# Attention and feed-forward kernel: more buffers for attention, and the first feed-forward chunk placed ahead of the second batch's attention

## The chip, the cores and the metric

The kernel runs on one core of one Trainium2 chip. The metric is device microseconds (us) of one execution. The clock that was granted to the tensor engine and the busy times come from a profile of one execution; the span in a profile is about 1.7 us shorter than the time of the same run.

## The reference

Four batches of eight heads, 768 tokens and 64 features go through attention that keeps four sink tokens and a window of 128. The heads are then joined to 512 features per token, and a gated feed-forward block with RMS norm follows.

```python
scores = scale * np.matmul(q, k.transpose(0, 1, 3, 2))
keep = is_sink | in_window                      # first 4 keys, or 0 <= query - key < 128
a = softmax(np.where(keep, scores, -1e9))
x = (a @ v).transpose(0, 2, 1, 3).reshape(B * S, H * D)      # 3072 x 512

xn = x / np.sqrt(np.mean(x * x, -1, keepdims=True) + 1e-6) * rms_g
g, val = xn @ w_gate, xn @ w_val                # 512 -> 1536
out = (g * sigmoid(g) * val) @ w_out            # 1536 -> 512
```

## The kernel before

Attention works on pairs of heads, four pairs to a batch. The feed-forward part works on 12 chunks of 256 tokens, three to a batch. Inputs are float32 in memory and are cast to bf16 by the loads; all those loads are issued by GpSimd, in one queue. A list scheduler puts the instructions of each engine in a fixed order, by the order in which the program emits them and by what each needs. On its engine each instruction then waits its turn.

```python
ld = ctx.enter_context(tc.tile_pool(name="ld", bufs=2))     # q, k as loaded
c1 = ctx.enter_context(tc.tile_pool(name="c1", bufs=2))     # qT, kT
vp = ctx.enter_context(tc.tile_pool(name="vp", bufs=3))     # v with a column of ones
ptp = ctx.enter_context(tc.tile_pool(name="ptp", bufs=3))   # probabilities
# ...
def attention_pair(b, hp_idx):
    # ... load q, k (2 heads each) and v; transpose q and k on the tensor engine
    vaug = vp.tile([P, NT, D + 1], BF16, tag="vaug")
    nc.gpsimd.memset(vaug[:, :, D : D + 1], 1.0)
    nc.gpsimd.dma_start(out=vaug[:, :, 0:D], in_=vv)
    # ... scores into s_ps, exp on ScalarE, mask on VectorE, product with v into o_ps
    # ... divide by the sum: x_all[:, b * NT : (b + 1) * NT, h * D : (h + 1) * D]

def stats_batch(b):      # 6 blocks: bn_stats, bn_aggr; then mean square, Sqrt, reciprocal
    ...

def ffn_chunk(c):
    # ... xn = x_all * rstd; 8 transposes into xnT_ps; xnT = xnT_ps * rms_g
    hTs[0] = emit_silu(emit_gv(0))          # 4 gate and 4 value matmuls, then the gating
    hTs[1] = emit_silu(emit_gv(1))
    for f in range(NFB):                    # 12 blocks
        if f + 2 < NFB:
            hTs[f + 2] = emit_silu(emit_gv(f + 2))
        emit_out(f, hTs.pop(f))             # 2 matmuls with wo

attention_batch(0)
stats_batch(0)
load_weights()                              # wg, wv, wo: one GpSimd load each
for b in range(1, B):
    attention_batch(b)
    stats_batch(b)
    ffn_batch(b - 1)
ffn_batch(B - 1)
```

The softmax here doesn't subtract the row's maximum and nothing guards it: scores larger than these inputs give would overflow.

Of the kernel before, what the change touches and what calls it, by code (L numbers as in the profile page):

```python
# [10 lines left out]
FP32 = mybir.dt.float32  # L11
BF16 = mybir.dt.bfloat16
ACT = mybir.ActivationFunctionType
ALU = mybir.AluOpType
# [3 lines left out]
def kernel(  # L18
# [33 lines left out]
    assert S % TC == 0  # L52
    TPC = TC // P
    CPB = S // TC
    SCALE = 1.0 / float(D) ** 0.5
    EPS = 1e-6

# [66 lines left out]
    x_all = xpool.tile([P, TBLK, DM], FP32)  # L124

    ld = ctx.enter_context(tc.tile_pool(name="ld", bufs=2))
    c1 = ctx.enter_context(tc.tile_pool(name="c1", bufs=2))
    vp = ctx.enter_context(tc.tile_pool(name="vp", bufs=3))
    ptp = ctx.enter_context(tc.tile_pool(name="ptp", bufs=3))
    smallp = ctx.enter_context(tc.tile_pool(name="smallp", bufs=3))  # L130
    apS = ctx.enter_context(tc.tile_pool(name="apS", bufs=2, space=bass.MemoryType.PSUM))
    apO = ctx.enter_context(tc.tile_pool(name="apO", bufs=1, space=bass.MemoryType.PSUM))
# [5 lines left out]
    fps = ctx.enter_context(tc.tile_pool(name="fps", bufs=3, space=bass.MemoryType.PSUM))  # L138
    fpo = ctx.enter_context(tc.tile_pool(name="fpo", bufs=1, space=bass.MemoryType.PSUM))

    def attention_pair(b: int, hp_idx: int):
        h0 = 2 * hp_idx
        q_b16 = ld.tile([P, NT, 2, D], BF16, tag="qb")
        k_b16 = ld.tile([P, NT, 2, D], BF16, tag="kb")
        for hh in range(2):
            qv = q[b, h0 + hh].rearrange("(t p) d -> p t d", p=P)
            kv = k[b, h0 + hh].rearrange("(t p) d -> p t d", p=P)
            nc.gpsimd.dma_start(out=q_b16[:, :, hh, :], in_=qv)  # L148
            nc.gpsimd.dma_start(out=k_b16[:, :, hh, :], in_=kv)  # L149

        make_consts()
        vaugs = []
        for hh in range(2):
            vv = v[b, h0 + hh].rearrange("(t p) d -> p t d", p=P)
# [3 lines that stand above are left out]
            vaugs.append(vaug)  # L158

        qT_ps = apS.tile([P, NT * P], BF16, tag="sps")  # L160
        for t in range(NT):
            nc.tensor.transpose(  # L162
                qT_ps[:, t * P : (t + 1) * P],
                q_b16[:, t, :, :].rearrange("p hh d -> p (hh d)"),
                ident[:],
            )
        qT2 = c1.tile([P, NT * P], BF16, tag="qT")
        nc.vector.tensor_copy(out=qT2[:], in_=qT_ps[:])
        kT_ps = apS.tile([P, NT * P], BF16, tag="sps")
        for t in range(NT):  # L170
            nc.tensor.transpose(  # L171
                kT_ps[:, t * P : (t + 1) * P],
                k_b16[:, t, :, :].rearrange("p hh d -> p (hh d)"),
                ident[:],
            )
        kT2 = c1.tile([P, NT * P], BF16, tag="kT")
        nc.vector.tensor_copy(out=kT2[:], in_=kT_ps[:])

        far = (NT - 2) * P
        pts, ptsinks = [], []  # L180
        for hh in range(2):
            pb = hh * D
            qT = qT2[pb : pb + D, :]
            kT = kT2[pb : pb + D, :]
            ssk_ps = apS.tile([NS, far], FP32, tag="sps")
            nc.tensor.matmul(  # L186
                ssk_ps[:],
                lhsT=kT[:, 0:NS],
                rhs=qT[:, 2 * P : NT * P],
                start=True,  # L190
                stop=True,
            )
            ptsink = ptp.tile([P, far], BF16, tag="ptsink")
            nc.gpsimd.memset(ptsink[:], 0.0)  # L194
            nc.scalar.activation(out=ptsink[0:NS, :], in_=ssk_ps[:], func=ACT.Exp, scale=SCALE)  # L195
            ptsinks.append(ptsink)
            pt_all = ptp.tile([P, NT * 2 * P], BF16, tag="ptall")
            pts.append(pt_all)

        for kp in range(KPAIRS):  # L200
            kb0 = 2 * kp
            nkb = 2 if kb0 + 1 < NT else 1
            spp = []
            for hh in range(2):
                pb = hh * D
                qT = qT2[pb : pb + D, :]
                kT = kT2[pb : pb + D, :]
                s_ps = apS.tile([P, 4 * P], FP32, tag="sps")
                cols = 0
                for i in range(nkb):  # L210
                    kb = kb0 + i
                    ncols = 2 * P if kb < NT - 1 else P
                    nc.tensor.matmul(  # L213
                        s_ps[:, i * 2 * P : i * 2 * P + ncols],
                        lhsT=kT[:, kb * P : (kb + 1) * P],
                        rhs=qT[:, kb * P : kb * P + ncols],
                        start=True,
                        stop=True,
                    )
                    cols = i * 2 * P + ncols  # L220
                spp.append((s_ps, cols))
            mk = maskA if kp == 0 else maskB
            for hh in range(2):
                s_ps, cols = spp[hh]
                base = kb0 * 2 * P
                nc.scalar.activation(  # L226
                    out=pts[hh][:, base : base + cols],
                    in_=s_ps[:, 0:cols],
                    func=ACT.Exp,
                    scale=SCALE,  # L230
                )
                nc.vector.tensor_tensor(  # L232
                    out=pts[hh][:, base : base + cols],
                    in0=pts[hh][:, base : base + cols],
                    in1=mk[:, 0:cols],
                    op=ALU.mult,
                )

        for hh in range(2):
            h = h0 + hh  # L240
            pt_all = pts[hh]
            ptsink = ptsinks[hh]
            vaug = vaugs[hh]
            o_ps = apO.tile([P, NT, D + 1], FP32, tag="ops")
            for jq in range(NT):
                nc.tensor.matmul(  # L246
                    o_ps[:, jq, :],
                    lhsT=pt_all[:, jq * 2 * P : jq * 2 * P + P],
                    rhs=vaug[:, jq, :],
                    start=True,  # L250
                    stop=(jq == 0),
                )
                if jq >= 1:
                    nc.tensor.matmul(  # L254
                        o_ps[:, jq, :],
                        lhsT=pt_all[:, (jq - 1) * 2 * P + P : jq * 2 * P],
                        rhs=vaug[:, jq - 1, :],
                        start=False,
                        stop=(jq == 1),
                    )  # L260
                if jq >= 2:
                    nc.tensor.matmul(  # L262
                        o_ps[:, jq, :],
                        lhsT=ptsink[:, (jq - 2) * P : (jq - 1) * P],
                        rhs=vaug[:, 0, :],
                        start=False,
                        stop=True,
                    )
            r = smallp.tile([P, NT, 1], FP32, tag="recip")
            nc.vector.reciprocal(out=r[:], in_=o_ps[:, :, D : D + 1])  # L270
            nc.vector.tensor_tensor(
                out=x_all[:, b * NT : (b + 1) * NT, h * D : (h + 1) * D],
                in0=o_ps[:, :, 0:D],
                in1=r[:].to_broadcast((P, NT, D)),
                op=ALU.mult,
            )

    def attention_batch(b: int):
        for hp_idx in range(H // 2):
            attention_pair(b, hp_idx)  # L280

    rstd_all = xpool.tile([P, TBLK, 1], FP32)

    def stats_batch(b: int):
        mv = fsm.tile([P, NT, nc.vector.BN_AGGR_DIM], FP32, tag="mv")
        for t in range(NT):
            stats = fsm.tile([P, nc.vector.BN_STATS_DIM], FP32, tag="stats")
            nc.vector.bn_stats(out=stats[:], in_=x_all[:, b * NT + t, :])  # L288
            nc.vector.bn_aggr(out=mv[:, t, :], in_=stats[:])
        msq = fsm.tile([P, NT, 1], FP32, tag="msq")  # L290
        nc.vector.tensor_tensor(
            out=msq[:], in0=mv[:, :, 0:1], in1=mv[:, :, 0:1], op=ALU.mult
        )
        nc.vector.tensor_tensor(out=msq[:], in0=msq[:], in1=mv[:, :, 1:2], op=ALU.add)
        nc.vector.tensor_scalar_add(out=msq[:], in0=msq[:], scalar1=EPS)
        nc.scalar.activation(out=msq[:], in_=msq[:], func=ACT.Sqrt)
        nc.vector.reciprocal(out=rstd_all[:, b * NT : (b + 1) * NT, :], in_=msq[:])

    def ffn_chunk(c: int):
        tb0 = c * TPC  # L300
# [25 lines left out]
        def emit_gv(f):  # L326
            gv_ps = fps.tile([P, 2, TC], FP32, tag="gv")
            for kci in range(NKC):
                nc.tensor.matmul(  # L329
                    gv_ps[:, 0, :],  # L330
                    lhsT=wg_bf[:, kci, f * P : (f + 1) * P],
                    rhs=xnT[:, kci, :],
                    start=(kci == 0),
                    stop=(kci == NKC - 1),
                )
            for kci in range(NKC):
                nc.tensor.matmul(  # L337
                    gv_ps[:, 1, :],
# [51 lines left out]
            r0 = row0 + tbi * P  # L390
            nc.sync.dma_start(out=out[r0 : r0 + P, :], in_=o_sb[:])

    def ffn_batch(b: int):
        for sub in range(CPB):
            ffn_chunk(b * CPB + sub)

    attention_batch(0)
    stats_batch(0)
    load_weights()
    for b in range(1, B):  # L400
        attention_batch(b)
        stats_batch(b)
        ffn_batch(b - 1)
    ffn_batch(B - 1)


# [33 lines left out]
```

## Time and profile before

| Reading of the kernel before | value | view |
|---|---|---|
| time, median of the first 3 runs | 334.79 us (333.09 to 336.43) | runs |
| span of the profiled run | 331.0 us | page |
| tensor engine busy | 286.6 us, 87% | page, part 1 |
| idle for the q of batch 1 | 8.43 us | timeline |
| that q, from issue to landing | 17.0 us | chain of waits |
| first gate matmul of chunk 0 | 60.42 us | timeline |
| attention of batch 1 with chunk 0 | 60.42 to 100.05 us, 39.6 us | timeline |
| one chunk alone | 16.83 us | timeline |

These are lines of the profile page. Part 1 gives the busy time of each engine (PE is the tensor engine, PEld its loading of weights, DVE the vector engine, ACT ScalarE, POOL GpSimd, each with its count of instructions). Part 2 cuts the span into 40 slices of 8.3 us and gives the busy tenths of each; PEclk is the clock that was granted to the tensor engine, in tenths of full speed.

```profile
PE 286.6 (87%) x2432; PEld 186.9 (56%) x2432; DVE 227.5 (69%) x616; ACT 146.6 (44%) x309; POOL 102.2 (31%) x186
...
PE   1687641999987999999988999999779999999993
...
PEclk9999999999999999999999999999999999999998
DMA  7999999979968010399890010931010101010101
```

After the seventh slice the tensor engine is nearly full. The 4 and the 1 in slices six and seven are the hole that the change is aimed at, and the DMA line shows the queues nearly full until then. The hole itself is seen in the timeline of the tensor engine. Its columns are start, length, operation, output and inputs, sizes, count, and in brackets the idle time before the line and what ended it.

```profile
47.30 0.24 PE L262 MATMUL o_ps<-vaug,ptsink 128*128 128x65 bf16 x1
55.97 0.80 PE L162 MATMUL qT_ps<-ident,q_b 128*128 128x128 bf16 x6 [8.43 <-DMA q_b<-in_q_dram]
...
58.68 1.24 PE L311 MATMUL xnT_ps<-ident,xn 128*128 128x128 bf16 x8
60.42 1.01 PE L329 MATMUL gv_ps<-xnT,wg_bf 128*128 128x256 bf16 x4 [0.49 <-DVE xnT L318]
```

Attention of batch 0 ends at 47.5 us. The next instruction in the fixed order transposes a q that has not landed. Only behind it come the transposes of chunk 0 (xnT_ps) and its first gate matmul. Why that q is late shows in the timeline of GpSimd, which issues the loads.

```profile
24.97 0.86 POOL L113 DMA_DIRECT2D wg_bf<-in_moe_w_gate_dram  x1
...
27.99 0.12 POOL L156 MEMSET vaug<- 128x6 bf16 x1 [0.83 <-PE o_ps L262]
...
29.31 0.76 POOL L116 DMA_DIRECT2D wv_bf<-in_moe_w_val_dram  x1
34.91 0.12 POOL L156 MEMSET vaug<- 128x6 bf16 x1 [4.84 <-PE o_ps L262]
...
36.23 1.02 POOL L119 DMA_DIRECT2D wo_bf<-in_moe_w_out_dram  x1
...
38.86 0.86 POOL L148 DMA_DIRECT2D q_b<-in_q_dram  x1
```

GpSimd twice stops for a v buffer, until the tensor engine has finished with an old one (o_ps). With three buffers the last v loads of batch 0, and everything behind them, are issued late and among the weights. The list of loads gives size and time from issue to landing.

```profile
wg_bf<-in_moe_w_gate_dram POOLq DMA_DIRECT2D x1, 1536.0 KB, 12.1
wv_bf<-in_moe_w_val_dram POOLq DMA_DIRECT2D x1, 1536.0 KB, 16.4
wo_bf<-in_moe_w_out_dram POOLq DMA_DIRECT2D x1, 1536.0 KB, 17.7
```

The weights land at 37.1, 45.7 and 53.9 us, 8.6 and 8.2 us apart, with v loads of batch 0 between them in the queue, and q of batch 1 lands right behind them, at 55.8 us. In the chain of waits (start, length, what) it is one piece.

```profile
38.86 16.97 DMA q_b<-in_q_dram
```

Last, matmuls of one size (256 columns) in three windows: 24 to 32 us, inside attention of batch 0 and long before the hole, then 60 to 67 us and 70 to 80 us. The columns after the count are busy time, mean nanoseconds of one, and idle time before.

```profile
L213 PE MATMUL s_ps<-qT,kT 64*128 64x256 bf16 x8 | 2.4, 394 | 1.8 <-ACT pt_all L226 1.8
...
L329 PE MATMUL gv_ps<-xnT,wg_bf 128*128 128x256 bf16 x8 | 2.4, 404 | 0.5 <-DVE xnT L318 0.5
...
L213 PE MATMUL s_ps<-qT,kT 64*128 64x256 bf16 x14 | 2.9, 273 | 0.3 <-ACT ptsink L195 0.2
L329 PE MATMUL gv_ps<-xnT,wg_bf 128*128 128x256 bf16 x12 | 2.3, 275 | 0.0
```

After the hole a gate matmul takes 404 ns, later 275 ns.

### The profile page before, as it was taken

How to read it: one execution, taken by the hardware profiler on the slowest of the kernel's cores; microseconds unless marked ns; L12 is line 12 of the kernel's file. 1: busy time of each engine (PE TensorE's matmuls, PEld its weight loads, DVE VectorE, ACT ScalarE, POOL GpSimd, SP SyncE). 2: the span in 40 equal slices, each digit the busy share in tenths (PEclk: the TensorE clock that was granted, in tenths of full speed). 3: DMA queues.
4: the chain of work that ended last, by engine and by line, in shares of the span. 5: the costliest groups of instructions: out<-in, count | busy, mean ns of one | idle time of the engine just before them, and what ended most of it. 6: DMA issues, size and time to landing. Idle time of an engine off the chain costs nothing.

```text
span 331.0 us, 6385 instructions
## 1 busy us (share of the span) xinstructions
PE 286.6 (87%) x2432; PEld 186.9 (56%) x2432; DVE 227.5 (69%) x616; ACT 146.6 (44%) x309; POOL 102.2 (31%) x186
## 2 busy tenths in 40 slices
PE   1687641999987999999988999999779999999993
PEld 1243321365565767655756677655557676767771
DVE  0354455677798686797887776987966767676662
ACT  0654340567636253466454353666343333242422
POOL 8995644477751000487430000830000000000000
PEclk9999999999999999999999999999999999999998
DMA  7999999979968010399890010931010101010101
GB/s 48 71 98 168 205 203 170 78 51 81 75 42 107 2 63 2 71 103 78 57 107 5 2 63 0 137 28 12 2 65 0 63 2 63 3 64 2 63 2 63
DMA packets 81886, 20.86 MB, mean 63 GB/s; under 512 B 76224, under 2 KB 77760, under 8 KB 81856
## 3 DMA queue, kind: packets, MB, share of 16 engines
q0 software_dynamic: 77872, 14.16, 52.9%
q1 hardware_dynamic: 3984, 6.30, 5.2%
q8 instruction: 19, 0.31, 0.4%
q14 instruction: 11, 0.09, 0.1%
HBM read 28.31 MB, written 6.29 MB: 105 GB/s over the span
## 4 chain that ended last, share of the span: by engine, by line
PE 51%; DVE 23%; ACT 10%; DMA 6%; POOL 4%; issue 3%; ACTq 0%; POOLq 0%
PE gv_ps L329 11%; PE gv_ps L337 10%; PE out_ps L371 10%; DVE hT L359 9%; DVE u_sb L350 9%; PE s_ps L213 9%; ACT t_sb L348 7%; DMA q_b<-in_q_dram 6%; DVE stats L288 3%; PE o_ps L246 3%; ACT ptsink L195 2%; PE qT_ps L162 2%; PE kT_ps L171 2%; PE ssk_ps L186 2%; PE o_ps L254 2%
## 5 line engine op out<-in xcount | busy, mean ns | idle before, releaser
L348 ACT ACTIVATE t_sb<-gv_ps 128x256 bf16<-128x256 f32 x144 | 55.0, 384 | 108.3 <-DVE hT L359 70.5
L329 PE MATMUL gv_ps<-xnT,wg_bf 128*128 128x256 bf16 x576 | 92.7, 275 | 2.2 <-DVE xnT L318 2.0
L371 PE MATMUL out_ps<-wo_bf,hT 128*128 128x512 bf16 x288 | 86.0, 380 | 6.5 <-DVE hT L359 5.9
L337 PE MATMUL gv_ps<-xnT,wv_bf 128*128 128x256 bf16 x576 | 90.8, 274 | 0.0
L350 DVE SCALAR_TENSOR_TENSOR u_sb<-t_sb,gv_ps 128x256 bf16<-128x256 bf16 x144 | 59.9, 418 | 44.5 <-ACT t_sb L348 44.0
L329 PEld LDWEIGHTS <-wg_bf 128*128 128x128 bf16 x576 | 54.4, 98 | 35.0 <-issue 7.6
L359 DVE SCALAR_TENSOR_TENSOR hT<-u_sb,gv_ps 128x256 bf16<-128x256 bf16 x144 | 59.7, 418 | 3.4
L337 PEld LDWEIGHTS <-wv_bf 128*128 128x128 bf16 x576 | 55.3, 98 | 9.7 <-issue 3.5
L226 ACT ACTIVATE pt_all<-s_ps 128x512 bf16<-128x512 f32 (+1 forms) x96 | 52.8, 562 | 14.7 <-PE s_ps L213 13.3
L213 PE MATMUL s_ps<-qT,kT 64*128 64x256 bf16 x192 | 40.1, 301 | 9.4 <-ACT ptsink L195 5.1
L371 PEld LDWEIGHTS <-hT 128*128 128x128 bf16 x288 | 25.8, 98 | 19.3 <-DVE hT L359 12.7
L156 POOL MEMSET vaug<- 128x6 bf16 x32 | 4.8, 152 | 96.6 <-PE o_ps L262 96.6
L232 DVE TENSOR_TENSOR pt_all<-pt_all,maskB 128x512 bf16<-128x512 bf16 (+1 forms) x64 | 24.8, 390 | 12.3 <-ACT pt_all L226 11.4
L148 POOL DMA_DIRECT2D q_b<-in_q_dram x32 | 27.5, 859 | 18.0 <-PE qT_ps L162 12.0
L213 PEld LDWEIGHTS <-kT 64*128 64x128 bf16 x192 | 11.9, 97 | 32.0 <-issue 29.5
L149 POOL DMA_DIRECT2D k_b<-in_k_dram x32 | 27.3, 852 | 5.4 <-DMA wo_bf<-in_moe_w_out_dram 5.4
L246 PE MATMUL o_ps<-vaug,pt_all 128*128 128x65 bf16 x192 | 25.2, 209 | 2.6 <-DMA vaug<-in_v_dram 2.4
L157 POOL DMA_DIRECT2D vaug<-in_v_dram x32 | 26.9, 840 | 0.9 <-POOL ptsink L194 0.9
L195 ACT ACTIVATE ptsink<-ssk_ps 4x512 bf16<-4x512 f32 x32 | 17.5, 579 | 18.0 <-PE ssk_ps L186 17.8
L246 PEld LDWEIGHTS <-pt_all 128*128 128x128 bf16 x192 | 17.5, 105 | 14.0 <-DVE pt_all L232 5.8
L232 DVE TENSOR_TENSOR pt_all<-pt_all,maskA 128x512 bf16<-128x512 bf16 x32 | 13.6, 425 | 16.7 <-ACT pt_all L226 16.5
L254 PE MATMUL o_ps<-vaug,pt_all 128*128 128x65 bf16 x160 | 23.7, 207 | 0.0
(47 smaller groups left out, 247.1 us busy)
## 6 DMA issues: line engine op xcount, KB each, us to landing
out_dram<-o_sb SPq DMA_DIRECT2D x24, 256.0 KB, 2.2
q_b<-in_q_dram POOLq DMA_DIRECT2D x32, 96.0 KB, 3.3
k_b<-in_k_dram POOLq DMA_DIRECT2D x32, 96.0 KB, 3.4
vaug<-in_v_dram POOLq DMA_DIRECT2D x32, 96.0 KB, 3.3
wg_bf<-in_moe_w_gate_dram POOLq DMA_DIRECT2D x1, 1536.0 KB, 12.1
wv_bf<-in_moe_w_val_dram POOLq DMA_DIRECT2D x1, 1536.0 KB, 16.4
wo_bf<-in_moe_w_out_dram POOLq DMA_DIRECT2D x1, 1536.0 KB, 17.7
rmsg<-in_moe_rms_g_dram SPq DMA_DIRECT2D x1, 2.0 KB, 2.2
```

The source lines that it names most:

```text
L148: nc.gpsimd.dma_start(out=q_b16[:, :, hh, :], in_=qv)
L213: nc.tensor.matmul(s_ps[:, i * 2 * P : i * 2 * P + ncols], lhsT=kT[:, kb * P : (kb + 1) * P], rhs=qT[:, kb * P : kb * P + ncols], start=Tr ...
L226: nc.scalar.activation(out=pts[hh][:, base : base + cols], in_=s_ps[:, 0:cols], func=ACT.Exp, scale=SCALE,)
L232: nc.vector.tensor_tensor(out=pts[hh][:, base : base + cols], in0=pts[hh][:, base : base + cols], in1=mk[:, 0:cols], op=ALU.mult,)
L246: nc.tensor.matmul(o_ps[:, jq, :], lhsT=pt_all[:, jq * 2 * P : jq * 2 * P + P], rhs=vaug[:, jq, :], start=True, stop=(jq == 0),)
L254: nc.tensor.matmul(o_ps[:, jq, :], lhsT=pt_all[:, (jq - 1) * 2 * P + P : jq * 2 * P], rhs=vaug[:, jq - 1, :], start=False, stop=(jq == 1),)
L329: nc.tensor.matmul(gv_ps[:, 0, :], lhsT=wg_bf[:, kci, f * P : (f + 1) * P], rhs=xnT[:, kci, :], start=(kci == 0), stop=(kci == NKC - 1),)
L337: nc.tensor.matmul(gv_ps[:, 1, :], lhsT=wv_bf[:, kci, f * P : (f + 1) * P], rhs=xnT[:, kci, :], start=(kci == 0), stop=(kci == NKC - 1),)
L348: nc.scalar.activation(out=t_sb[:], in_=gv_ps[:, 0, :], func=ACT.Tanh, scale=0.5)
L350: nc.vector.scalar_tensor_tensor(out=u_sb[:], in0=t_sb[:], scalar=1.0, in1=gv_ps[:, 1, :], op0=ALU.add, op1=ALU.mult,)
L359: nc.vector.scalar_tensor_tensor(out=hT[:], in0=u_sb[:], scalar=0.5, in1=gv_ps[:, 0, :], op0=ALU.mult, op1=ALU.mult,)
L371: nc.tensor.matmul(out_ps[:, tbi, :], lhsT=hT[:, tbi * P : (tbi + 1) * P], rhs=wo_bf[:, f, :], start=(f == 0), stop=(f == NFB - 1),)
```

## The change

The intent is to let attention of batch 0 run without waiting for buffers, and to fill the hole with chunk 0, which needs no q. Three edits carry it. The pools get 4 and 9 buffers, so that all of batch 0's v loads can be issued ahead of the weights. Chunk 0 is emitted before attention of batch 1, and an ordering edge puts the tensor engine's work for attention of batch 1 behind the first gate matmul of chunk 0's sixth block. The statistics of batch 0 are taken in two parts of 2 and 4 blocks, so that chunk 0 (2 blocks) could start earlier. The diff also cuts the attention function into three functions, which does the same work and is left out here.

```diff
-    c1 = ctx.enter_context(tc.tile_pool(name="c1", bufs=2))
-    vp = ctx.enter_context(tc.tile_pool(name="vp", bufs=3))
-    ptp = ctx.enter_context(tc.tile_pool(name="ptp", bufs=3))
+    c1 = ctx.enter_context(tc.tile_pool(name="c1", bufs=HP))          # 4
+    vp = ctx.enter_context(tc.tile_pool(name="vp", bufs=H + 1))       # 9
+    ptp = ctx.enter_context(tc.tile_pool(name="ptp", bufs=H + 1))     # 9
 ... (attention_pair cut into three functions; statistics for any range of blocks)
-                nc.tensor.matmul(
+                mm = nc.tensor.matmul(
                     gv_ps[:, 0, :], ...
                 )
+                first_gv.append(mm)
 ...
     attention_batch(0)
-    stats_batch(0)
+    stats_blocks(0, TPC)
+    stats_blocks(TPC, NT - TPC)
     load_weights()
+    first_gv = []
+    ffn_chunk(0)
     for b in range(1, B):
-        attention_batch(b)
+        if b == 1:
+            with tc.issue_after(first_gv[5 * NKC].ins):
+                attention_batch(b)
+        else:
+            attention_batch(b)
         stats_batch(b)
-        ffn_batch(b - 1)
-    ffn_batch(B - 1)
+        ... (the chunks of batch b - 1 except chunk 0; after the loop those of batch B - 1)
```

In the built order of the tensor engine all of chunk 0 but its last two matmuls, not only its first five blocks, stands ahead of batch 1's attention. The chunk that then shares its time with attention of batch 1 is chunk 1.

More of the change, by code (lines that the diff above doesn't have):

```diff
@@ L54 @@
     CPB = S // TC
+    HP = H // 2
     SCALE = 1.0 / float(D) ** 0.5
@@ L139, with attn_front @@
     fpo = ctx.enter_context(tc.tile_pool(name="fpo", bufs=1, space=bass.MemoryType.PSUM))
-    def attention_pair(b: int, hp_idx: int):
+    def attn_front(b: int, hp_idx: int):
         h0 = 2 * hp_idx
@@ L198, in attention_pair, with attn_kps @@
             pts.append(pt_all)
-        for kp in range(KPAIRS):
+        return dict(
+            b=b, h0=h0, qT2=qT2, kT2=kT2, vaugs=vaugs, pts=pts, ptsinks=ptsinks
+        )
+    def attn_kps(st, kp_list):
+        qT2, kT2, pts = st["qT2"], st["kT2"], st["pts"]
+        for kp in kp_list:
             kb0 = 2 * kp
@@ L237, in attention_pair @@
                 )
-        for hh in range(2):
-            h = h0 + hh
-            pt_all = pts[hh]
-            ptsink = ptsinks[hh]
-            vaug = vaugs[hh]
-            o_ps = apO.tile([P, NT, D + 1], FP32, tag="ops")
-            for jq in range(NT):
-                nc.tensor.matmul(
-                    o_ps[:, jq, :],
-                    lhsT=pt_all[:, jq * 2 * P : jq * 2 * P + P],
-                    rhs=vaug[:, jq, :],
-                    start=True,
-                    stop=(jq == 0),
-                )
-                if jq >= 1:
-                    nc.tensor.matmul(
-                        o_ps[:, jq, :],
-                        lhsT=pt_all[:, (jq - 1) * 2 * P + P : jq * 2 * P],
-                        rhs=vaug[:, jq - 1, :],
-                        start=False,
-                        stop=(jq == 1),
-                    )
-                if jq >= 2:
-                    nc.tensor.matmul(
-                        o_ps[:, jq, :],
-                        lhsT=ptsink[:, (jq - 2) * P : (jq - 1) * P],
-                        rhs=vaug[:, 0, :],
-                        start=False,
-                        stop=True,
-                    )
-            r = smallp.tile([P, NT, 1], FP32, tag="recip")
-            nc.vector.reciprocal(out=r[:], in_=o_ps[:, :, D : D + 1])
-            nc.vector.tensor_tensor(
-                out=x_all[:, b * NT : (b + 1) * NT, h * D : (h + 1) * D],
-                in0=o_ps[:, :, 0:D],
-                in1=r[:].to_broadcast((P, NT, D)),
-                op=ALU.mult,
-            )
@@ L278, in attention_batch, with attn_O_write @@
-    def attention_batch(b: int):
-        for hp_idx in range(H // 2):
-            attention_pair(b, hp_idx)
+    def attn_O_write(st, hh, jq0, njq):
+        b = st["b"]
+        h = st["h0"] + hh
+        pt_all = st["pts"][hh]
+        ptsink = st["ptsinks"][hh]
+        vaug = st["vaugs"][hh]
+        o_ps = apO.tile([P, njq, D + 1], FP32, tag="ops")
+        for j in range(njq):
+            jq = jq0 + j
+            nc.tensor.matmul(
+                o_ps[:, j, :],
+                lhsT=pt_all[:, jq * 2 * P : jq * 2 * P + P],
+                rhs=vaug[:, jq, :],
+                start=True,
+                stop=(jq == 0),
+            )
+            if jq >= 1:
+                nc.tensor.matmul(
+                    o_ps[:, j, :],
+                    lhsT=pt_all[:, (jq - 1) * 2 * P + P : jq * 2 * P],
+                    rhs=vaug[:, jq - 1, :],
+                    start=False,
+                    stop=(jq == 1),
+                )
+            if jq >= 2:
+                nc.tensor.matmul(
+                    o_ps[:, j, :],
+                    lhsT=ptsink[:, (jq - 2) * P : (jq - 1) * P],
+                    rhs=vaug[:, 0, :],
+                    start=False,
+                    stop=True,
+                )
+        r = smallp.tile([P, njq, 1], FP32, tag="recip")
+        nc.vector.reciprocal(out=r[:], in_=o_ps[:, :, D : D + 1])
+        tb0 = b * NT + jq0
+        nc.vector.tensor_tensor(
+            out=x_all[:, tb0 : tb0 + njq, h * D : (h + 1) * D],
+            in0=o_ps[:, :, 0:D],
+            in1=r[:].to_broadcast((P, njq, D)),
+            op=ALU.mult,
+        )
@@ L282, with stats_blocks @@
+    def attention_batch(b: int):
+        for hp_idx in range(HP):
+            st = attn_front(b, hp_idx)
+            attn_kps(st, list(range(KPAIRS)))
+            for hh in range(2):
+                attn_O_write(st, hh, 0, NT)
     rstd_all = xpool.tile([P, TBLK, 1], FP32)
-    def stats_batch(b: int):
-        mv = fsm.tile([P, NT, nc.vector.BN_AGGR_DIM], FP32, tag="mv")
-        for t in range(NT):
+    def stats_blocks(tb0: int, nb: int):
+        mv = fsm.tile([P, nb, nc.vector.BN_AGGR_DIM], FP32, tag="mv")
+        for t in range(nb):
@@ L287, in stats_batch @@
             stats = fsm.tile([P, nc.vector.BN_STATS_DIM], FP32, tag="stats")
-            nc.vector.bn_stats(out=stats[:], in_=x_all[:, b * NT + t, :])
+            nc.vector.bn_stats(out=stats[:], in_=x_all[:, tb0 + t, :])
             nc.vector.bn_aggr(out=mv[:, t, :], in_=stats[:])
-        msq = fsm.tile([P, NT, 1], FP32, tag="msq")
+        msq = fsm.tile([P, nb, 1], FP32, tag="msq")
         nc.vector.tensor_tensor(
@@ L296, in stats_batch @@
         nc.scalar.activation(out=msq[:], in_=msq[:], func=ACT.Sqrt)
-        nc.vector.reciprocal(out=rstd_all[:, b * NT : (b + 1) * NT, :], in_=msq[:])
+        nc.vector.reciprocal(out=rstd_all[:, tb0 : tb0 + nb, :], in_=msq[:])
+    def stats_batch(b: int):
+        stats_blocks(b * NT, NT)
     def ffn_chunk(c: int):
@@ L328, in emit_gv @@
             for kci in range(NKC):
-                nc.tensor.matmul(
+                mm = nc.tensor.matmul(
                     gv_ps[:, 0, :],
@@ L391, in ffn_chunk @@
             nc.sync.dma_start(out=out[r0 : r0 + P, :], in_=o_sb[:])
-    def ffn_batch(b: int):
-        for sub in range(CPB):
-            ffn_chunk(b * CPB + sub)
     attention_batch(0)
-    stats_batch(0)
+    stats_blocks(0, TPC)
+    stats_blocks(TPC, NT - TPC)
     load_weights()
+    first_gv = []
+    ffn_chunk(0)
     for b in range(1, B):
-        attention_batch(b)
-        stats_batch(b)
-        ffn_batch(b - 1)
-    ffn_batch(B - 1)
+        if b == 1:
[3 more added lines that the diff above has]
+            attention_batch(b)
+        stats_batch(b)
+        for c in range(CPB):
+            if (b - 1) * CPB + c > 0:
+                ffn_chunk((b - 1) * CPB + c)
+    for c in range(CPB):
+        ffn_chunk((B - 1) * CPB + c)
 _INS = ['q', 'k', 'v', 'n_sink', 'window', 'moe_w_gate', 'moe_w_val', 'moe_w_out', 'moe_rms_g']
```

## The prediction

> **What bounds the kernel now.** From 60.4 us (first gate matmul) on the tensor engine is nearly full: the windows view gives it 37.1 of 39.6 us in the first merged stage (attention of batch 1 with chunk 0), 20.4 of 20.5 us later. A chunk alone repeats every 16.8 us in the chain of waits. The loss lies before: in the timeline attention of batch 0 ends on the tensor engine at 47.5 us, then the engine waits 8.4 us for q of batch 1, whose transposes stand, in the built order, ahead of chunk 0. That q was issued at 38.9 and took 17.0 us to land, behind the three weight loads (landed 37.1, 45.7, 53.9; about 8.2 us each). Two v loads of batch 0 queued behind weights too, because their 3 buffers came free late (issues at 28.5 and 35.4; two waits of 1.2 us); the fourth pair took about 14.5 us to its last x_all write, the second about 12.
>
> **What the change does.** (1) With 9 buffers, all v loads of batch 0 are issued before the weights. The weights are then issued together at about 30 us (before: 25, 29, 36) and, at 8.2 us each less the v traffic, the last lands at about 55. Attention of batch 0 should end near 44 instead of 48.4 us. (2) Chunk 0 stands whole ahead of batch 1's attention; its 16.8 us fill the time in which q of batch 1 is on its way. (3) Splitting the first statistics adds one square root and three vector operations (0.2 us each); the vector engine still does nearly all six blocks (4.9 us) first, so it gains little. (4) Later stages keep the same work and nearly the same order.
>
> **Sum, in the profiled span.** Statistics end near 49, first gate matmul near 51.5. The clock matters: matmuls of the same gate form took 404 ns at 60 to 67 us and 275 ns at 70 to 80. The Trainium skill ("TensorE: Matmul & The Clock Gate", the HAM clock gate) says an idle array runs at half clock until about 3.4 us of sustained work; the two durations agree in direction. Chunk 0 thus starts slow, about 5 us for its first three blocks, until 56.5, by when the output weights have landed; nine more at 1.3 us plus the last outputs end it near 69.5. After transposes and q and k copies chunk 1 begins near 72, now with a warm clock. The merged stage that took 39.6 us loses about 3 us of slow clock and ends near 109. What followed it before (331 - 100 = 231 us) is one lone chunk shorter: 214. Total about 323.5 against 331, a gain of 7.5 us, 2.2%. On the median of 334.8: **327.2 us**, 8 in 10 between 323 and 331. Chances: faster by over 2% 0.58, within 2% 0.41, slower by over 2% 0.01.
>
> **What would show it.** Right: no long wait of a q transpose on a DMA at 48 to 56 us; chunk 0 alone from about 51 to 70; attention of batch 0 done near 44; merged stage about 36.5 us; the last five chunks unchanged at 16.8 us. Wrong: the first output matmul waits for its weights past 58 us; chunk 0 starts later than 54; the merged stage stays near 40 us; a later stage stretches.
>
> **What would make it wrong.** Weights landing later than 57 us, since they are issued later; chunk 0 staying slow throughout; pairs of batch 2, now prefetched in one lone chunk instead of two, costing more than the 5 us each read from the stages before. Upward: the first part of the statistics letting chunk 0 start before 49 us.

## The result, and the profile after

The kernel after took 325.55 us, the median of 12 runs (324.82 to 328.04). The kernel before, in the same rounds and the first ones, took 335.75 us, the median of 15 (332.78 to 336.63). The ratio is 0.972, with a 95% interval of 0.970 to 0.975: faster.

The page of the kernel after (profiled run: 326.67 us, span 325.0 us). The runs of both kernels fall into two groups, those of the kernel before some 3 us apart. This run is one of the slower group of the kernel after, while the profiled run of the kernel before (332.75 us) is one of its faster group; the section on repeats comes back to this.

```profile
PE 285.0 (88%) x2432; PEld 186.2 (57%) x2432; DVE 227.7 (70%) x620; ACT 147.2 (45%) x310; POOL 101.8 (31%) x186
...
PE   1588817999999799999899999999789999999993
...
PEclk9999999999999799999999999999999999999998
```

The tensor engine does the same work (2432 matmuls, 285 us), with a smaller hole: 1 and 7 in slices six and seven in place of 4 and 1. Its slices are now 8.1 us. There is a new 7 in the row of the granted clock, in the fourteenth slice; it comes up again below. The timeline of the tensor engine:

```profile
49.24 1.07 PE L326 MATMUL xnT_ps<-ident,xn 128*128 128x128 bf16 x8 [6.36 <-DVE xn L322]
50.75 1.44 PE L344 MATMUL gv_ps<-xnT,wg_bf 128*128 128x256 bf16 x6 [0.44 <-DVE xnT L333]
51.98 0.95 PE L353 MATMUL gv_ps<-xnT,wv_bf 128*128 128x256 bf16 x4
...
53.86 0.60 PE L353 MATMUL gv_ps<-xnT,wv_bf 128*128 128x256 bf16 x4
55.86 0.59 PE L387 MATMUL out_ps<-wo_bf,hT 128*128 128x512 bf16 x2 [1.40 <-DMA wo_bf<-in_moe_w_out_dram]
...
68.47 0.50 PE L163 MATMUL qT_ps<-ident,q_b 128*128 128x128 bf16 x6
...
69.77 0.61 PE L326 MATMUL xnT_ps<-ident,xn 128*128 128x128 bf16 x8
```

Chunk 0 starts at 50.75 us instead of 60.42. Until its end at 69.8 us it shares the engine only with the first transposes of batch 1, which take q at 68.47 us without a wait. Two things still hold chunk 0: 6.36 us for the statistics on the vector engine, and 1.40 us for the output weights wo. Four matmuls in a row take 0.95 us at 51.98 us and 0.60 us at 53.86 us: the slow start is still there, but shorter. On GpSimd the loads now go out like this:

```profile
28.91 0.88 POOL L114 DMA_DIRECT2D wg_bf<-in_moe_w_gate_dram  x1
29.66 0.87 POOL L117 DMA_DIRECT2D wv_bf<-in_moe_w_val_dram  x1
30.39 1.16 POOL L120 DMA_DIRECT2D wo_bf<-in_moe_w_out_dram  x1
31.40 0.97 POOL L149 DMA_DIRECT2D q_b<-in_q_dram  x1
...
33.02 0.98 POOL L149 DMA_DIRECT2D q_b<-in_q_dram  x1
```

All v loads of batch 0 went out before the weights. The two loads of q for the first pair of batch 1, one per head, went out right behind the weights; the second landed 24.7 us after its issue, at 57.7 us, more than 10 us before it is taken. Attention of batch 0 finished at 43.7 us instead of 48.4 us. In the chain of waits the piece that was q is now wo:

```profile
30.39 25.43 DMA wo_bf<-in_moe_w_out_dram
```

The windows view gives the stretch of chunk 0, then the merged stage (attention of batch 1 with chunk 1). Each row has the window, its length, the busy time of each engine with the count of instructions, the granted clock, the time that DMA packets took as a share of the DMA engines' time (it can exceed 1), and GB/s.

```profile
50.70:70.90 20.20, 18.52 (x143) 13.36 (x142) 12.40 (x32) 5.69 (x14) 13.34 (x27) 1.00 1.54 123
70.90:107.40 36.50, 33.77 (x351) 20.14 (x349) 30.96 (x89) 22.80 (x45) 24.84 (x43) 1.00 1.12 83
```

The merged stage lasts 36.5 us; before it was 39.6 us. Where the 6.0 us between the profiles come from can be read off at one point, the start of the chunk after the merged stage. Before, that was chunk 1 at 100.05 us; after, it is chunk 2 at 107.39 us, with one chunk of 16.8 us more done. The lead at that point is 100.05 + 16.83 - 107.39 = 9.5 us. At the end it is 6.0 us, so 3.5 us were lost again. By the chunks' transposes, 3.0 us of that are lost before chunk 5 (187.78 us before, 181.28 us after) and about 0.5 us later.

### The profile page after: what moved, and what is told of

It is laid out like the page before. It is cut to its first block, busy times and chain, and to the rows that moved or that the text cites. A ratio compares the mean times of both kernels' runs of the same rounds, so it can differ in the third digit from the quotient of the medians. Undisturbed runs are those within 1.5% of the kernel's fastest.

```text
span 325.0 us, 6376 instructions
## 1 busy us (share of the span) xinstructions
PE 285.0 (88%) x2432; PEld 186.2 (57%) x2432; DVE 227.7 (70%) x620; ACT 147.2 (45%) x310; POOL 101.8 (31%) x186
## 4 chain that ended last, share of the span: by engine, by line
PE 46%; DVE 23%; ACT 9%; DMA 8%; POOL 8%; issue 4%; ACTq 0%; POOLq 0%
PE gv_ps L344 11%; PE out_ps L387 11%; PE gv_ps L353 10%; DVE u_sb L366 9%; DVE hT L375 8%; DMA wo_bf<-in_moe_w_out_dram 8%; PE s_ps L219 7%; ACT t_sb L364 7%; DVE stats L300 3%; PE o_ps L254 2%; ACT ptsink L196 2%; POOL q_b L149 2%; POOL k_b L150 2%; POOL vaug L158 2%; PE ssk_ps L187 1%
## 5 line engine op out<-in xcount | busy, mean ns | idle before, releaser
L219 PE MATMUL s_ps<-qT,kT 64*128 64x256 bf16 x192 | 38.7, 294 | 5.8 <-ACT ptsink L196 4.2
L270 PE MATMUL o_ps<-vaug,ptsink 128*128 128x65 bf16 x128 | 18.7, 206 | 0.0
```

The source lines that it names most:

```text
L219: nc.tensor.matmul(s_ps[:, i * 2 * P : i * 2 * P + ncols], lhsT=kT[:, kb * P : (kb + 1) * P], rhs=qT[:, kb * P : kb * P + ncols], start=Tr ...
```

## The experiments

The theory: chunk 0 in the time in which q is on its way makes the gain, and the buffers add to it by ending attention of batch 0 sooner. The rivals: the buffers do most of it alone; an earlier load of q would do as well; or the slow start after the hole is the real cost, so that keeping the engine busy would do as well. In the following, "before" beside a time is the median of the kernel before in the same rounds on the same chip.

### The buffers alone

```diff
-    c1 = ctx.enter_context(tc.tile_pool(name="c1", bufs=2))
-    vp = ctx.enter_context(tc.tile_pool(name="vp", bufs=3))
-    ptp = ctx.enter_context(tc.tile_pool(name="ptp", bufs=3))
+    c1 = ctx.enter_context(tc.tile_pool(name="c1", bufs=H // 2))
+    vp = ctx.enter_context(tc.tile_pool(name="vp", bufs=H + 1))
+    ptp = ctx.enter_context(tc.tile_pool(name="ptp", bufs=H + 1))
```

> The kernel before with only the deeper buffers (projections 4, v 9, probabilities 9), order of stages unchanged. Theory A (the gain comes from chunk 0 standing ahead of batch 1's attention): attention of batch 0 ends near 44 us as in the changed kernel, but the first q transpose of batch 1 still waits, now about 14 us, until its q lands at 57 to 58 us behind the weights; total about 336 to 337 us, ratio 1.000 to 1.006. Rival B (the gain comes from the early v loads): ratio at most 0.985.

Measured: 331.45 us, before 335.93, ratio 0.989 (0.982 to 0.995). The expectation of no gain missed. Its mechanism was there, in the timeline of the tensor engine:

```profile
58.17 0.80 PE L162 MATMUL qT_ps<-ident,q_b 128*128 128x128 bf16 x6 [15.40 <-DMA q_b<-in_q_dram]
```

The wait for q grew from 8.43 to 15.40 us, as expected, and the first gate matmul came 1.1 us later (61.53 us). But the profiled span was 329.5 us against 331.0 us. After the longer wait seven gate matmuls ran in a row, and the engine reached full speed at 62.9 us, where the kernel before, with pieces of attention between its gate matmuls, ran slowly until about 68 us; chunk 1's transposes came at 94.60 instead of 96.11 us. That explains 1.5 of the 4.5 us between the medians. The rest agrees with what the section on repeats finds, that the kernel before is in its slower group in most runs; no experiment shows that the buffers cause this.

### The order alone, with the old buffers

The edit is told against the kernel after.

```diff
-    c1 = ctx.enter_context(tc.tile_pool(name="c1", bufs=HP))
-    vp = ctx.enter_context(tc.tile_pool(name="vp", bufs=H + 1))
-    ptp = ctx.enter_context(tc.tile_pool(name="ptp", bufs=H + 1))
+    c1 = ctx.enter_context(tc.tile_pool(name="c1", bufs=2))
+    vp = ctx.enter_context(tc.tile_pool(name="vp", bufs=3))
+    ptp = ctx.enter_context(tc.tile_pool(name="ptp", bufs=3))
```

> The changed kernel with the old buffers (2, 3, 3). Theory A: attention of batch 0 ends at 48.4 us as before, statistics at 53.5, first gate matmul near 55.5, chunk 0 ends near 73 instead of 69.2, no long wait on q; total about 329 to 330 us, ratio 0.980 to 0.985. Rival B: ratio 0.995 or more.

Measured: 330.47 us, before 335.93, ratio 0.986 (0.981 to 0.991), within half a microsecond of the expectation. Gate matmuls start at 55.99 us, earlier than in the kernel before (60.42 us) but later than in the kernel after (50.75 us), because attention of batch 0 ends as late as before. By the medians, order alone gives 5.5 us, buffers alone 4.5 us, both together 10.2 us, nearly the sum. But the medians mix two groups of runs (see the repeats). By the profiled spans, order alone gives 331.0 - 328.5 = 2.5 us, buffers alone 1.5 us, both together 6.0 us, though the profiled run of both is of the slower group of its kernel: there the two together give more than the sum. These are single profiles, but it fits the timelines, where the buffers alone only lengthen the wait for q. Either way neither part is the whole, and the rival that the buffers do most of it falls.

### q, k and v of the first pair of batch 1 loaded ahead of the weights

Against the kernel before, with the new buffers as well:

```diff
+    early = {}
+    def load_qkv(b, hp_idx): ...        # the loads, cut out of attention_pair
+        return q_b16, k_b16, vaugs
     def attention_pair(b, hp_idx):
+        q_b16, k_b16, vaugs = early.pop((b, hp_idx), None) or load_qkv(b, hp_idx)
 ...
     stats_batch(0)
+    early[(1, 0)] = load_qkv(1, 0)
     load_weights()
```

> The kernel before with deeper buffers, stage order unchanged, and q, k, v of batch 1's first pair issued ahead of the weights instead of behind them. If the wait on q behind the weights is what was lost, this is another cure of it: first q transpose of batch 1 at about 36 to 41 us without a long wait, weights about 5 us later (last at 60 to 61), total 328 to 331 us, ratio 0.977 to 0.986. If what counts is that chunk 0's matmuls fill the time of the load whatever is waited for, the later weights give a new wait of about 8 us and the ratio stays above 0.995.

Measured: 329.06 us, before 335.93, ratio 0.981 (0.976 to 0.986), inside the expectation. The q transposes ran at 40.55 us without a wait. A new wait of 4.30 us on the q of the next pair, at 62.52 us, took part of it back: it moved the wait from one pair to the next. So an earlier load is worth 2.4 us over the buffers alone (331.45 us), where the order of the change is worth 5.9 us over them (325.55 us).

### Keeping the tensor engine busy while it waits for q

Against the kernel before: 28 matmuls on constants, whose result nobody reads, behind the last product of batch 0.

```diff
 ... (last_o, which holds the last product of attention, is left out)
+        if b == 1 and hp_idx == 0:
+            w_ps = fps.tile([P, 2, TC], FP32, tag="gv")
+            with tc.issue_after(last_o[0].ins):
+                for _ in range(NWARM):                  # 28
+                    nc.tensor.matmul(w_ps[...], lhsT=ident[:], rhs=maskB[:], start=True, stop=True)
```

> The kernel before with 28 extra matmuls of 128x512 on constants, issued behind the last matmul of batch 0's attention, so that the tensor engine is busy through most of its 8.4 us wait for q. Nothing waits for them and they should be over before q lands at 56 us. Clock theory: the first matmuls of the merged stage run at 275 ns instead of 404 ns; the stage (first gate matmul of chunk 0 to that of chunk 1) takes about 37 instead of 39.6 us; ratio 0.990 to 0.994. If the clock at that place costs nothing: stage 39.6 us, ratio 1.000.

Measured: 334.09 us, before 335.93, ratio 0.996 (0.989 to 1.002), no difference clear of the noise. The first gate matmuls were fast, as meant. The slow stretch only moved, though, as the windows view of 2 us each shows; the number behind the five engines is the granted clock.

```profile
60.00:62.00 2.00, 1.18 (x10) 0.74 (x11) 2.00 (x7) 1.53 (x3) 2.00 (x3) 1.00 1.90 121
...
64.00:66.00 2.00, 2.00 (x11) 0.63 (x10) 0.81 (x2) 1.11 (x2) 0.00 (x0) 0.50 0.28 18
66.00:68.00 2.00, 2.00 (x16) 1.08 (x15) 1.17 (x4) 1.34 (x4) 0.00 (x0) 0.50 0.00 0
```

The filling matmuls ended at 56.4 us; between 56 and 62 us the engine was busy 3.4 of 6 us, with the short pieces that wait for copies, and from 62 us the clock was halved. In this run filling the wait did not cure the slow stretch, as sparse work followed. That rival gets no support; but as the slow stretch only moved, this run does not measure what it costs.

### The kernel before, three times more

These runs are the unchanged kernel, one profile each, to see what parts its runs into groups.

> The kernel before, unchanged, to get a second profile: its runs fall into two groups, 332.8 to 334.2 us with a granted clock of 0.996 and 334.8 to 336.9 us with 0.990 to 0.994, and the first profile (332.75 us) is of the first group. If the second group has a stretch of half clock, this profile (4 chances in 5 of it) shows a slice with a granted clock well below 1 after 60 us and matmuls of the same gate form near 404 ns there, about 3 us lost against the first profile. If the groups differ by something else, the clock column is as in the first profile and the difference lies in waits.

> The kernel before once more for a profile of its slower group (334.8 to 336.9 us, granted clock 0.990 to 0.994); both profiles so far fell in the faster group. If it is of the slower group: a stretch with a granted clock near 0.5 somewhere after 60 us and about 3 us lost there. If it is of the faster group again, nothing new.

> As the third look: the kernel before, for a profile of its slower group; half clock in one or two stretches after 60 us if the clock is what sets the groups apart.

Measured: 333.32, 336.23 and 335.92 us. The first is of the faster group, like the profiled run of before (332.75 us), and shows nothing new. The other two are of the slower group, and their profiles differ from the first two in two places, beside a small shift of the start. First, the slow stretch goes on longer: from chunk 0's to chunk 1's transposes it takes 38.7 and 38.2 us, against 37.4 us in both profiles of the faster group. Second, the clock is halved once in the stage after the statistics of batch 1, here in the window of 102 to 107 us of the third repeat:

```profile
102.00:107.00 5.00, 4.80 (x26) 3.10 (x25) 3.12 (x13) 2.74 (x5) 0.66 (x1) 0.66 1.18 162
```

From chunk 1's to chunk 2's transposes it takes 23.1 us instead of 21.6 us. From there on all profiles agree, and between the third repeat and the first profile the total is 312.02 - 308.51 = 3.5 us at the last chunk. Of these, 0.8 us were there before chunk 0 (59.46 against 58.68 us), and the repeat of the faster group has 0.6 us of that too. So the third repeat lost 1.2 us in the slow stretch and 1.5 us in one spell of half clock; the fourth lost 0.8 and 1.5 us. By their times, 3 of the first 15 runs of the kernel before are clearly in the faster group (332.8 to 333.2 us) and 10 in the slower (335.4 to 336.6 us), with two between. Of the kernel after, 8 of 12 took 324.8 to 325.6 us and 4 took 326.6 to 328.0 us. Between the means of the faster groups the change gains 333.0 - 325.3 = 7.7 us.

### One part of statistics instead of two

Against the kernel after:

```diff
-    stats_blocks(0, TPC)
-    stats_blocks(TPC, NT - TPC)
+    stats_batch(0)
```

> The changed kernel with the statistics of batch 0 in one piece again. My reading: the split gives nothing, since the vector engine does all six blocks first either way and the first output matmul waits for its weights until about 55.8 us in any case; time 325 to 326 us as the changed kernel, ratio to before 0.970 to 0.975. Rival (the split lets chunk 0 start early): 1.5 us slower or more, ratio 0.977 or more.

Measured: 325.87 us, before 336.69, ratio 0.970 (0.966 to 0.974), as expected: the same as the kernel after. The split gives nothing, because the vector engine still does the statistics of nearly all six blocks before it turns to chunk 0. Chunk 0 starts 0.7 us later here (51.46 us), but the first output matmul then finds its weights landed, at 56.30 us against 55.86 us.

This run also shows what the spell of half clock costs the kernel after, because its profile has none. The lines of the tensor engine at the end of the merged stage, first in the kernel after, then in this one:

```profile
105.42 0.60 PE L387 MATMUL out_ps<-wo_bf,hT 128*128 128x512 bf16 x2 [0.72 <-DVE hT L375]
107.39 0.37 PE L344 MATMUL gv_ps<-xnT,wg_bf 128*128 128x256 bf16 x1 [1.36 <-DVE xnT L333]
107.80 1.03 PE L387 MATMUL out_ps<-wo_bf,hT 128*128 128x512 bf16 x2
```

```profile
105.86 0.61 PE L387 MATMUL out_ps<-wo_bf,hT 128*128 128x512 bf16 x2 [0.72 <-DVE hT L375]
107.83 0.27 PE L344 MATMUL gv_ps<-xnT,wg_bf 128*128 128x256 bf16 x1 [1.36 <-DVE xnT L333]
108.24 0.60 PE L387 MATMUL out_ps<-wo_bf,hT 128*128 128x512 bf16 x2
```

Order and waits are the same to 0.01 us, yet in the first run the pair of matmuls takes 1.03 us, and in the second 0.60 us. From chunk 2's first gate matmul to chunk 5's transposes it takes 73.89 us in the first and 72.48 us in the second: the spell costs 1.4 us. Nearly the same stall stands in the profiles of the kernel before and of most versions; whether the clock falls there differs from run to run.

### Without the ordering edge

Against the kernel after:

```diff
-        if b == 1:
-            with tc.issue_after(first_gv[5 * NKC].ins):
-                attention_batch(b)
-        else:
-            attention_batch(b)
+        attention_batch(b)
```

> The changed kernel without the ordering edge, so that in the built order the q and k transposes of batch 1 stand behind the first 24 gate and value matmuls of chunk 0 instead of behind all of it. Q lands at 57 to 58 us, the output weights at 55.8: one wait of about 2 us more in chunk 0, given back in part because the transposes need not be done at its end. 325.5 to 327.5 us, ratio 0.972 to 0.978. If the edge is what makes the gain: ratio 0.985 or more.

Measured: 328.8 us, before 336.69, ratio 0.976 (0.971 to 0.982). The edge is worth about 3 us, more than expected: 2.9 us against the version with one part of statistics, which ran in the same rounds and equals the kernel after, and every run here is slower than every run there. Without it the q transposes stand behind 24 matmuls of chunk 0 and wait again:

```profile
57.86 0.80 PE L163 MATMUL qT_ps<-ident,q_b 128*128 128x128 bf16 x6 [2.94 <-DMA q_b<-in_q_dram]
```

The wait alone is not the whole of it. After it the granted clock is 0.62 in the window of 60 to 65 us. One run of four, with a clock of 1.0, took 327.01 us; the other three 328.6 to 329.9 us.

### Weights in halves, and the rest of the statistics later

Against the kernel after: six loads of half a weight each, so that chunk 0's first six blocks need only the first halves; the statistics of the last four blocks are held behind chunk 0's own scaling; the edge stands at block 10.

```diff
 ... (the weight tiles cut in halves, and their use in the matmuls, are left out)
+        for i in range(NWS):                            # 2 halves of the 1536
+            fs = slice(i * FW, (i + 1) * FW)
+            nc.gpsimd.dma_start(out=wg_bf[i][:], in_=g_v[:, :, fs])
+            nc.gpsimd.dma_start(out=wv_bf[i][:], in_=v_v[:, :, fs])
+            nc.gpsimd.dma_start(out=wo_bf[i][:], in_=o_v[:, i * FPW : (i + 1) * FPW, :])
 ...
-    stats_blocks(TPC, NT - TPC)
     load_weights()
     ffn_chunk(0)
+    with tc.issue_after(last_xnT[0].ins):
+        stats_blocks(TPC, NT - TPC)
 ...
-            with tc.issue_after(first_gv[5 * NKC].ins):
+            with tc.issue_after(first_gv[10 * NKC].ins):
```

> The changed kernel with each weight loaded in two halves (gate, value, output of the first six blocks, then the rest), the statistics of blocks 2 to 5 held behind chunk 0's last scaled transpose, and the ordering edge moved to block 10. If the first output matmul's wait for its weights (55.8 us) and the 5 us of statistics ahead of chunk 0 are what now sets its start: first gate matmul near 48, first output matmul near 52, chunk 0 over near 65.5 instead of 69.2; 321 to 322.5 us, ratio 0.958 to 0.963. If something else limits it, no faster than the changed kernel (0.972).

Measured: 323.91 us, before 336.69, ratio 0.964 (0.960 to 0.968). By the medians, which are of different rounds, this beats the kernel after by 1.6 us (and the version with one part of statistics, of the same rounds, by 2.0 us), less than was expected. Chunk 0 starts at 48.64 us, 2.1 us earlier, and no longer waits for wo. But its first 20 matmuls ran slowly (407 to 418 ns in the mean), until about 52.8 us, and the first output matmul came at 53.47 us; the expectation of the run with 14 filling matmuls, below, says 24 and 53.4 us, but the last four took 272 ns. Besides, ScalarE loaded the table of the square root and then that of tanh again in the middle of the chunk (1.28 us each, at 53.85 and 55.37 us), which cost the tensor engine a stall of 0.67 us.

### Filling matmuls on the kernel after, and on the version above

Against each: constants multiplied (18 and 14 times) between the end of attention of batch 0 and chunk 0.

```diff
     stats_blocks(0, TPC)
 ... (load_weights() and, on the kernel after, the rest of the statistics; last_o is left out as above)
+    w_ps = fps.tile([P, 2, TC], FP32, tag="gv")
+    with tc.issue_after(last_o[0].ins):
+        for _ in range(NWARM):                          # 18; 14 on the version above
+            nc.tensor.matmul(w_ps[...], lhsT=ident[:], rhs=maskB[:], start=True, stop=True)
```

> The changed kernel with 18 extra matmuls of 128x512 on constants during the 6.4 us in which the tensor engine waits for the statistics ahead of chunk 0. Its first gate matmuls then run at the fast clock, but the first output matmul still waits for its weights until about 55.9 us, so nothing is gained: 325 to 326.5 us, ratio 0.968 to 0.975. If the slow clock at the start of chunk 0 is what sets its end: 323.5 to 324.5 us.

> The kernel with split weights and late statistics (first output matmul at 53.5 us there, not at 52, because its first 24 matmuls ran at the slow clock until 53.4), with 14 extra matmuls in the wait for the statistics. Here nothing else holds the first output matmul, so the clock should count: first output matmul near 51.5, chunk 0 over near 66; 321.5 to 322.5 us, ratio 0.957 to 0.961. If the clock is not it: 323.9 us, ratio 0.964.

Measured for the first: 327.05 us, before 334.33, ratio 0.978 (0.969 to 0.988); no gain over the kernel after, and the median lies 0.5 us above the expected range. The second: 323.60 us (323.33 to 323.67), before 334.33, ratio 0.966 (0.960 to 0.972), the fastest measured, but only 0.3 us under the version above, and less than was expected. In both the slow start is gone, and another wait has taken its place, first the weights, then the vector engine:

```profile
55.54 0.59 PE L389 MATMUL out_ps<-wo_bf,hT 128*128 128x512 bf16 x2 [1.84 <-DMA wo_bf<-in_moe_w_out_dram]
```

```profile
52.90 0.60 PE L394 MATMUL out_ps<-wo,hT 128*128 128x512 bf16 x2 [1.46 <-DVE hT L382]
```

In the kernel after, the wait for wo was 1.40 us and ended at 55.86 us. Fast matmuls reach it sooner and wait longer, 1.84 us. In the version with halves, the late statistics stand on the vector engine ahead of the gating that makes hT. At this point three limits lie within about 2 us of each other, by these waits: the clock, the weights and the vector engine.

## Why the prediction was right

The predicted time of 327.2 us was 1.6 us high; the result lies in the range and on the side that was held likeliest. Point by point:

- **Attention of batch 0 done near 44 us.** It was 43.7 us.
- **Weights issued together near 30 us, the last landing near 55 us.** They were issued at 28.9 to 30.4 us, and the last landed at 30.39 + 25.43 = 55.8 us.
- **Statistics end near 49, first gate matmul near 51.5 us.** It was 50.75 us. That the split gains little was right too: one part instead of two took 325.87 us.
- **Three slow blocks until 56.5 us, output weights landed by then.** The clock rose earlier, near 53 us, and the blocks ended at 54.5 us. But the first output matmul then waited 1.40 us for its weights, until 55.86 us, so the sum came out nearly the same. That the two errors cancel was luck. That the time was set by the weights is confirmed by the filling matmuls, which took away the slow start there and gained nothing.
- **Chunk 0 done near 69.5 us, no q wait.** Its last output matmuls started at 69.16 us and ended at about 69.8 us, and q was taken at 68.47 us without a wait.
- **Merged stage about 36.5 us.** It was 36.5 us, ending at 107.4 us instead of the predicted 109 us.
- **The remainder, 214 us.** This is the term that was mis-sized: it took 325.0 - 107.4 = 217.6 us. A spell of half clock after the statistics costs 1.4 us of it (the run with one part of statistics does without it and takes 324.0 - 107.83 = 216.2 us). Of the other 2.1 us, 1.6 us are lost before chunk 5. The prediction had named this risk: pairs of batch 2 are prefetched beside one lone chunk instead of two. That this is the cause was not tested by itself.
- **The last five chunks unchanged.** In both kernels the transposes of the last four chunks are 16.83 us apart (for the last two, 291.68 and 308.51 us before, 285.64 and 302.47 us after).

The mechanism held: chunk 0 covers the wait for q. The sum came out well in part by luck, because the merged stage ended 1.6 us earlier than predicted while the remainder took 3.6 us longer, 1.4 us of it the spell of half clock.

The predicted gain of 7.6 us agrees with the 7.7 us between the faster groups of runs. The measured medians differ by 10.2 us. What the prediction left out, and what makes the rest of the difference by these groups, is that the kernel before is in its slower group in most of its runs, and the kernel after in one of three; the profile it was built on was of the faster group. Two profiles of the slower group showed what such a run loses. Why the kernel before is tripped more often stays open, and so does the part of the gain of the buffers alone that its profile does not explain.

## What to carry to other kernels

Where an in-order engine waits at the head of its queue for a load, look for work that is ready and place it ahead of the waiting instruction, and make sure by an explicit edge that the built order keeps it there; here the edge alone was worth 3 us. Filling a wait with useless work to keep the clock up gave no gain clear of the noise: in the kernel before the slow stretch only moved, and in the other two runs the next wait, for weights or for another engine, took up the time. Before costing a change, look whether the runs of the kernel fall into groups and which group the profile is from: here 10.2 us by the medians are 7.7 us between the faster groups.

## What the Trainium skill lacked or had wrong

- "TensorE: Matmul & The Clock Gate", Part 1, gives about 3.4 us of sustained work as the time until the full clock. The runs agree that matmuls are slow first (404 against 275 ns), but the slow stretch, counted from the first transposes after the idle time, lasted from 3.5 us (kernel after, 49.24 to about 52.8 us) over 6.6 us (order alone, 54.29 to about 60.9 us) to nearly 13 us in the kernel before, where attention was mixed in (55.97 to about 68.8 us). Nor did a high busy share in the profile suffice: the 256-column matmuls of the scores stayed at 391 to 396 ns, in means over 4 or 8 us, all through attention of batch 0, with the tensor engine busy 26.9 of 39 us (8 to 47 us), and matmuls at 404 ns from 60 to 67 us, with it busy 6.6 of 7 us. The page gives no busy share that suffices.
- The same page's closing table, "Why this matters for your kernels", warns of idle gaps over about 3 us. Here two idle gaps of 0.72 and 1.36 us, with two matmuls between them and 20 transposes ahead of them, were enough to halve the clock in one run and not in another of the same waits. Its remarks that the window runs freely, and that transposes do not count as busy in the same way (Part 4), fit this; no run separates them.
- "DMA: Bandwidth & Descriptors", "Anatomy of one DMA — SWDGE (gpsimd) path", fits a load as 2.0 us plus its bytes over 436 GB/s. By that, an estimate for a weight of 1536 KB is 5.6 us. Behind each other the casting weight loads landed 7.5 us apart in the kernel after (at 40.8, 48.3 and 55.8 us), and 8.6 and 8.2 us apart in the kernel before, with other loads between them; a load of 96 KB took 17.0 us when it stood behind them. The page doesn't say whether the bytes of a load that casts are those before or after the cast. By those before, the bytes' part of the same fit gives an estimate of 7.2 us, which is near the 7.5 us; by those after, 3.6 us.
- "Perfetto Trace Analysis" does not say that a slow stretch can go unseen in the column of the granted clock; no other page names the column, though "TensorE: Matmul & The Clock Gate" warns in Part 1 that recorded clock events have been unreliable. In the kernel before the column shows 1.00 from 60 to 67 us, where matmuls took 404 ns, and from 8 to 47 us; later spells of half clock do show there (0.50 and 0.66).
- "ScalarE: Activation LUTs", "What ACT_TABLE_LOAD costs", gives about 1283 ns for the load, and each took 1.28 us here. But its total of about 2.66 us for a switch, with a drain, is not seen: with halved weights, ScalarE's tanh ended at 53.83 us, the square root started at 55.15 us and ended at 55.35 us, and the next tanh started at 56.67 us, so each switch took 1.32 us.
